# Attention beside a local branch on one core: larger PV batches, a split side branch, spare matmuls and new issue estimates

## Chip, cores, metric

One core of one Trainium2 chip. The time is the device time of one execution in us; medians of several runs are given. Profiled spans are some 2 us shorter than the timed figure of the same run. Most comparisons below are ratios to the kernel before, timed in the same rounds on the same chip: the mean time of one kernel's fast runs over that of the other's, so not quite the ratio of the medians quoted. A run counts as fast if it lies within 1.5% of the fastest of its kernel in these rounds.

## The reference, cut to what matters

```python
# shortened; x: [1, 2048, 640], 32 heads of 20
def _A_ref(x, wqkv, wo):          # full softmax attention
    scores = einsum("bhqd,bhkd->bhqk", q, k) * scale
    o = einsum("bhqk,bhkd->bhqd", softmax(scores), v)
    return heads_joined(o) @ wo
def _B_ref(x, wqkv, wo):          # each position sees 8 taps: itself and every second one before it
    logits = einsum("bhsd,bhswd->bhsw", q, kg) * scale      # masked where the tap is before the start
    o = einsum("bhsw,bhswd->bhsd", softmax(logits), vg)
    return heads_joined(o) @ wo
g = sigmoid((x * gate_w).sum(-1, keepdims=True))
return g * _A_ref(x, A_wqkv, A_wo) + (1 - g) * _B_ref(x, B_wqkv, B_wo)
```

Full attention is cut into 2048 units: one head, 128 keys, 512 queries. Each unit is one score matmul (contraction 20, in a strip of 32 rows), a share of one exponential, and one PV matmul, the product of the exponentials with V (21 output columns, in a strip of 32). The rest, called side work here, is projections, the tap branch B and the output projection ("fold").

## The kernel before

A scheduler written in Python runs while the program is built. It keeps an estimated time per engine, books every instruction with an estimated duration, and so fixes the order on each engine. On the chip only that order and the semaphores remain. Each slot `s` has three units or two in turn, with one exponential over all of them; two slots are called a pair, and the time from one pair to the next its pitch. The head is the time up to about 98 us, in which ScalarE is starved, and the tail what follows the last exponential.

```python
SEM_LAT = 0.07
...
actc = lambda n: 0.18 + n * 0.8334e-3            # booked time of an activation
...
    T("pe", 0.26, fn, reads=..., writes=[("score", s % 2)])                    # scores of a slot
    T("pe", 0.06 + 0.22 * max(1, (len(units) + 2) // 4), fn, ..., accum=["obank"])   # PV
...
for s in range(NT + 6):
    ...
    qk(s); exp(s)
    if s >= hold:                                # PV, every slot, of what the slot two back made
        todo = []
        while next_pv < NU and tile_of[next_pv][0] <= min(s - 2, NT - 1) and len(todo) < 6:
            ...
            todo.append(next_pv); next_pv += 1
        if todo: pv(todo)
    lim = exps[s - 1].end if ... else sch.avail["act"]
    run_side(lim)                                # side work that ends, by the estimate, before lim
```

Side work is written as generators that take turns. They share two PSUM banks (`side`); three and two banks hold the scores, one (`obank`) the PV sums. `gen_b(u)` is the tap branch for 256 positions: Q, K and V projections, eight products on VectorE, sums on TensorE, softmax, and eight more products; unit `u` starts when `u - 1` is done.

## Time and profile before

| | kernel before |
|---|---|
| time | 1134 us, median of 3 runs (1119 to 1134) |
| time of the execution that was profiled | 1115.7 us, not one of these three |
| profiled span, mean granted clock | 1113.9 us, 0.847 |
| first exponential starts, last one ends | 38.9 us, 1090.1 us |
| ScalarE: waits for scores | 93.6 us |

In the profile "us busy" and "idle before, releaser" per group of instructions are the columns to read; in the windows view each line is a stretch of the span, its length, the busy time and number of the instructions asked for, and the granted clock.

### The profile page before, as it was taken

To read this page: it belongs to the slowest core of one execution; us is meant where nothing else is said; L and a number is where in the kernel's file an instruction comes from. 1 tells how busy PE (TensorE), PEld (TensorE's weight loads), DVE (VectorE), ACT (ScalarE), POOL (GpSimd) and SP (SyncE) were. 2 spreads that over 40 slices of the span, in tenths; PEclk is the share of its full clock that TensorE was granted. 3 is DMA by queue.
4 is the path that set the end of the run, shared out by engine and by line. 5 is a ranking of instruction groups with operands and counts; after the bars stand their busy time and mean duration, and the time that the engine had idled before them with its cause. 6 is when DMAs were issued, how large, how long until landed. Compare 5 with 4: busy or idle time off the path is not lost.

```text
span 1113.9 us, 15049 instructions
## 1 busy us (share of the span) xinstructions
PE 1006.9 (90%) x6213; PEld 306.2 (27%) x6213; DVE 439.5 (39%) x772; ACT 960.8 (86%) x833; POOL 35.7 (3%) x26
## 2 busy tenths in 40 slices
PE   1678998999989999999999998989999989989997
PEld 0222322222323323422413332322112332322113
DVE  8315542334283542355461246364012255353102
ACT  0475999998898999998989999999998999998991
POOL 5000000004300000000000000000000000000000
PEclk9599998888898989977969997988568998976657
DMA  6310000000000000000000000000000000000000
GB/s 168 124 39 1 1 1 1 1 2 1 1 1 1 1 1 13 13 1 1 1 1 6 19 1 1 1 1 1 1 1 11 15 1 1 1 1 1 0 1 24
DMA packets 17216, 12.75 MB, mean 11 GB/s; under 512 B 11900, under 2 KB 15868, under 8 KB 17148
## 3 DMA queue, kind: packets, MB, share of 16 engines
q1 hardware_dynamic: 6268, 9.18, 2.4%
q10 hardware_dynamic: 10880, 2.62, 1.1%
q8 instruction: 48, 0.79, 0.3%
q14 instruction: 20, 0.16, 0.0%
HBM read 6.55 MB, written 2.62 MB: 8 GB/s over the span
## 4 chain that ended last, share of the span: by engine, by line
PE 63%; ACT 20%; issue 8%; DVE 6%; ACTq 2%; DMA 1%; DVEq 0%
PE side L368 25%; ACT ebuf L743 19%; PE score L730 19%; PE obank L754 18%; ACTq L290 2%; DVE stage L518 2%; DMA xT<-in_A_x_dram 1%; PE side L574 1%; PE side L528 1%; DVE vA L430 1%; DVE kT L387 1%; DVE oTt L455 1%; DVE oNt L466 1%; DVE qabs L410 0%; DVE oTn L469 0%
## 5 line engine op out<-in xcount | busy, mean ns | idle before, releaser
L743 ACT ACTIVATE ebuf<-score 128x1536 bf16<-128x1536 f32 (+1 forms) x819 | 955.3, 1253 | 98.7 <-PE score L730 93.6
L730 PE MATMUL score<-qT,kT 32*128 32x512 bf16 x2048 | 372.3, 444 | 50.4 <-ACT ebuf L743 45.3
L754 PE MATMUL obank<-ebuf,vA 128*21 128x512 bf16 x2048 | 361.4, 443 | 9.5 <-DVE vA L430 8.8
L730 PEld LDWEIGHTS score<-qT,kT 32*128 32x128 bf16 x2048 | 80.5, 93 | 318.7 <-ACT ebuf L743 211.1
L368 PE MATMUL side<-xT,kvw 128*128 128x256 bf16 (+1 forms) x760 | 142.5, 311 | 27.7 <-DMA xT<-in_A_x_dram 26.8
L754 PEld LDWEIGHTS obank<-ebuf,vA 128*21 128x21 bf16 x2048 | 75.0, 90 | 239.5 <-issue 218.2
L455 DVE STREAM_TRANSPOSE oTt<-obank 128x512 f32<-128x512 f32 x32 | 22.9, 716 | 228.8 <-PE obank L754 228.8
L368 PEld LDWEIGHTS side<-xT,kvw 128*128 128x128 bf16 x760 | 63.5, 100 | 89.3 <-issue 66.9
L368 PE MATMUL side<-xT,WqP 128*128 128x512 bf16 x160 | 58.9, 445 | 0.2
L368 PE MATMUL side<-stage,ident 128*128 128x512 bf16 (+1 forms) x192 | 55.6, 395 | 0.0
L586 DVE TENSOR_TENSOR stage<-vB,repB 128x1280 bf16<-128x1280 bf16 x64 | 50.1, 821 | 1.1
L618 DVE CAST outsb<-side 128x512 bf16<-128x512 f32 (+1 forms) x32 | 15.5, 490 | 88.7 <-PE side L368 88.7
L368 PE MATMUL side<-woA_r,oTn 128*128 128x512 bf16 (+1 forms) x256 | 50.3, 306 | 0.0
L518 DVE TENSOR_TENSOR stage<-qB,kB 128x1280 bf16<-128x1280 bf16 x64 | 48.5, 818 | 0.2
L598 DVE TENSOR_TENSOR oB<-side,rB 128x512 bf16<-128x512 f32 (+1 forms) x24 | 14.4, 602 | 79.2 <-PE side L368 79.2
L387 DVE TENSOR_SCALAR kT<-side,onesrow 128x512 bf16<-128x512 f32 x32 | 23.8, 743 | 39.0 <-PE side L368 39.0
L368 PE MATMUL side<-woBp,oB 128*128 128x512 bf16 (+1 forms) x160 | 33.9, 314 | 3.8 <-DVE oTn L469 2.8
L430 DVE CAST vA<-side 128x320 bf16<-128x320 f32 x32 | 15.7, 490 | 46.6 <-PE side L368 46.6
L368 PE MATMUL side<-kvw,xT 128*128 128x320 bf16 x160 | 32.5, 327 | 0.0
L509 DVE CAST qB<-side 128x512 bf16<-128x512 f32 (+1 forms) x24 | 14.4, 601 | 43.6 <-PE side L368 43.6
L509 DVE CAST vB<-side 128x512 bf16<-128x512 f32 (+1 forms) x24 | 14.4, 601 | 36.6 <-PE side L368 35.6
L509 DVE CAST kB<-side 128x512 bf16<-128x512 f32 (+1 forms) x24 | 14.4, 602 | 35.0 <-PE side L368 35.0
(76 smaller groups left out, 429.5 us busy)
## 6 DMA issues: line engine op xcount, KB each, us to landing
out_dram<-outsb SPq DMA_DIRECT2D x16, 160.0 KB, 1.8
stage<-in_B_wqkv_dram SPq DMA_DIRECT2D x1, 2400.0 KB, 8.8
stage<-in_A_wqkv_dram SPq DMA_DIRECT2D x1, 1600.0 KB, 6.9
kvw<-in_A_wqkv_dram SPq DMA_DIRECT2D x1, 800.0 KB, 9.4
woA_r<-in_A_wo_dram SPq DMA_DIRECT2D x4, 200.0 KB
woBp<-in_B_wo_dram SPq DMA_DIRECT2D x5, 160.0 KB
xT<-in_A_x_dram ACTq DMA_TRANSPOSE x20, 2.8
gwT<-in_gate_w_dram SPq DMA_DIRECT2D x1, 1.2 KB, 10.0
```

The source lines that it names most:

```text
L290: T("act", 6.0 + 2 * tcc, lambda e, c=c, tcc=tcc: e.dma_start_transpose(xT[:, c, tcc * 512:(tcc + 1) * 512], x_v[tcc * 512:(tcc + 1) * 512 ...
L368: ins = e.matmul(o, l, r, start=(first and i == 0), stop=(last and i == n - 1), skip_group_check=True)
L387: t = T("dve", dvc(512), lambda e, b=b, tcc=tcc: e.tensor_scalar(kT[:, q, tcc * 512:(tcc + 1) * 512], side[b][:, :], onesrow[:, 0:1], None ...
L430: t = T("dve", dvc(320), lambda e, o=o, i=i: e.tensor_copy(o, i), reads=[("side", b), "vAones"], writes=[("vA", kb, half)])
L455: T("dve", dvc(512), lambda e: e.transpose(oTt[:, :], obank[:, :]), reads=["obank"], writes=["oTt"])
L509: t = T("dve", dvc(n * TOK), lambda e, o=o, i=i: e.tensor_copy(o, i), reads=[("side", b)], writes=[key])
L518: T("dve", dvc(CN * TOK, 2), lambda e, w=w, ks=ks: e.tensor_tensor(prodB(w), qB[:, :, :], ks, ALU.mult), reads=["qB", "kB"], writes=[("pro ...
L586: T("dve", dvc(CN * TOK, 2), lambda e, w=w, vs=vs, rr=rr: e.tensor_tensor(prodB(w), vs, rr, ALU.mult), reads=["vB", ("repB", w4)], writes= ...
L618: t = T("dve", dvc(c1 - c0), lambda e, ob=ob, b=b, c0=c0, c1=c1: e.tensor_copy(ob[:, c0:c1], side[b][:, 0:c1 - c0]), reads=[("side", b)], ...
L730: ins = e.matmul(sc[:, i * 512:(i + 1) * 512], kT[32 * j:32 * j + 32, q, kb * P:(kb + 1) * P], qT[g % 3][32 * j:32 * j + 32, :], start=Tru ...
L743: exps[s] = T("act", actc(512 * n), lambda e: e.activation(ebuf[s % NE][:, 0:512 * n], score[s % 2][:, 0:512 * n], ACTF.Exp, scale=SCALE), ...
L754: ins = e.matmul(obank[32 * j:32 * j + DV, :], vA[:, kb, g % NQ, j, :], ebuf[s % NE][:, i * 512:(i + 1) * 512], start=(kb == 0), stop=(kb ...
```

## The change

The intent was to take work and changes of mode off TensorE (PV in whole groups of four, every second slot), to plan with truer durations, to keep TensorE supplied (tap projections of the next unit beside the softmax of this one), and to keep its clock up where nothing else is left to do. For the last, a spare matmul, whose result nobody reads, is put in where the plan has room before `lim`, TensorE's booked load over the last 3.4 us is under 62%, and a side bank is free. By mode I mean which part of the array a group of matmuls uses: strips of rows (scores, 32\*128 on the page), strips of columns (PV, 128\*21, and tap sums) or all of it (128\*128). In the trace before, at full clock and without idle time, the next matmul starts a median 0.315 us after one of 512 columns if the mode differs between them, and 0.216 us after it if both use all of the array. The diff is cut and in places shortened.

```diff
-SEM_LAT = 0.07
+LAT = {"pe": 0.18, "act": 0.06, "dve": 0.08, "pool": 0.1, "sp": 0.1}
+SWITCH = 0.11                                    # booked when TensorE's mode changes
-    actc = lambda n: 0.18 + n * 0.8334e-3
+    actc = lambda n: 0.08 + n * 0.8334e-3
-        T("pe", 0.26, fn, reads=..., writes=[("score", s % 2)])
+        T("pe", 0.215, fn, reads=..., writes=[("score", s % 2)], mode="row")
-        T("pe", 0.06 + 0.22 * max(1, (len(units) + 2) // 4), fn, ..., accum=["obank"])
+        T("pe", 0.215 * ((len(units) + 3) // 4), fn, ..., accum=["obank"], mode="col")
+    def filler(limit):                           # spare matmuls
+        while sch.avail["pe"] + 0.32 <= limit and sch.load(3.4) < 0.62:
+            best = [b for b in range(2) if not bank_used[b] and bank_free[b] <= sch.avail["pe"]]
+            if not best:
+                return
+            b = best[0]
+            t = T("pe", 0.215, lambda e: e.matmul(side[b][:, :], ident[:, :], xT[:, 0, 0:512], ...), ...)
+            bank_free[b] = t.end
-        if s >= hold:
+        if s >= hold and (s % 2 == 0 or s >= NT):
-            while next_pv < NU and ... and len(todo) < 6:
+            while next_pv < NU and ... and len(todo) < 12:
...
+            while todo and len(todo) % 4 and todo[-1] % 64 != 63:
+                todo.pop(); next_pv -= 1
-        lim = exps[s - 1].end if ... else sch.avail["act"]
+        lim = (exps[s - 1].end if ... else sch.avail["act"]) + (0.3, 0.15)[s % 2]
         run_side(lim)
+        filler(lim)
-    def gen_b(u): projections, then taps
+    def gen_bproj(u): projections of u, while the taps of u - 1 run
+    def gen_b(u): taps
```

More of the change, by code (lines that the diff above doesn't have):

```diff
@@ L68, in __init__ @@
         self.n = 0
+        self.mode = None
+        self.busy = []
         self.dma_final = {}
@@ L75, in ready, with load, task @@
             assert st is not None and st[0] is not None, k
-            t = max(t, st[0].end)
-        return t + SEM_LAT
-    def task(self, stream, dur, fn, reads=(), writes=(), dma=False, accum=()):
+            t = max(t, st[0].end + LAT[st[0].stream])
+        return t
+    def load(self, span):
+        t1 = self.avail["pe"]
+        tot = 0.0
+        for a, b in reversed(self.busy):
+            if b <= t1 - span:
+                break
+            tot += b - max(a, t1 - span)
+        return tot / span
+    def task(self, stream, dur, fn, reads=(), writes=(), dma=False, accum=(), mode="full"):
         deps = {}
@@ L108, in task @@
             d.mark = True
-            start = max(start, d.end + SEM_LAT)
+            start = max(start, d.end + LAT[d.stream])
+        if stream == "pe":
+            self.busy.append((start, start + dur))
+            if mode != self.mode:
+                dur += SWITCH
+                self.mode = mode
         if dma:
@@ L353, in release @@
         bank_used[b] = False
-        bank_free[b] = t.end + SEM_LAT
+        bank_free[b] = t.end + LAT[t.stream]
     def mm_group(b, mms, reads, cost, first=True, last=True, per=1):
@@ L435, in gen_gate @@
     def gen_gate(qc):
+        while qc > 1 and not done.get(("fold", qc - 2)):
+            yield ("cond",)
         b = yield from bank()
@@ L482, in gen_bweights, with gen_bproj @@
         done["bw"] = True
-    def gen_b(u):
-        qc, hu = divmod(u, 2)
+    def gen_bproj(u):
         t0 = u * TOK
-        while not (done.get("bw") and done.get(("gate", qc)) and (u == 0 or done.get(("b", u - 1)))):
+        while not (done.get("bw") and (u == 0 or done.get(("bl", u - 1)))):
             yield ("cond",)
-        while hu == 0 and qc > 0 and not done.get(("fold", qc - 1)):
-            yield ("cond",)
-        if u > 0:
-            T("dve", 0.15, lambda e: e.tensor_copy(kB[:, :, 0:PADB], kB[:, :, TOK:TOK + PADB]), reads=["kB"], writes=["kB"])
-            T("dve", 0.15, lambda e: e.tensor_copy(vB[:, :, 0:PADB], vB[:, :, TOK:TOK + PADB]), reads=["vB"], writes=["vB"])
         dst = {0: (qB, 0, "qB"), 1: (kB, PADB, "kB"), 2: (vB, PADB, "vB")}
         for m in range(3):
+            while m == 2 and u > 0 and not done.get(("bp", u - 1)):
+                yield ("cond",)
+            if u > 0 and m > 0:
+                bb, key = ((kB, "kB"), (vB, "vB"))[m - 1]
+                T("dve", 0.15, lambda e, bb=bb: e.tensor_copy(bb[:, :, 0:PADB], bb[:, :, TOK:TOK + PADB]), reads=[key], writes=[key])
             for f0 in range(0, CN, 2):
@@ L510, in gen_b @@
                 release(b, t)
+            if m == 1:
+                done[("bqk", u)] = True
+        done[("bproj", u)] = True
+    def gen_b(u):
+        qc, hu = divmod(u, 2)
+        while not (done.get(("bqk", u)) and done.get(("gate", qc)) and (u == 0 or done.get(("b", u - 1)))):
+            yield ("cond",)
         b = yield from bank()
@@ L520, in gen_b @@
             for f in range(CN):
-                yield ("pe", 0.2, sch.ready(*[("prod", half * 4 + w4) for w4 in range(4)]))
+                yield ("pe", 0.11, sch.ready(*[("prod", half * 4 + w4) for w4 in range(4)]))
                 def fn(e, f=f, half=half, b=b):
@@ L531, in fn @@
                     return ins
-                T("pe", 0.2, fn, reads=[("prod", half * 4 + w4) for w4 in range(4)] + ["Sel"],
+                T("pe", 0.11, fn, reads=[("prod", half * 4 + w4) for w4 in range(4)] + ["Sel"], mode="col",
                   **({"writes": [("side", b)]} if (half == 0 and f == 0) else {"accum": [("side", b)]}))
+        done[("bl", u)] = True
         if u == 0:
@@ L555, in gen_b @@
         T("pe", mmc(512), lambda e, b=b: e.matmul(side[b][:, :], negRep[0:32, :], m2, start=False, stop=True, skip_group_check=True),
-          reads=["mB", "negRep"], accum=[("side", b)])
+          reads=["mB", "negRep"], accum=[("side", b)], mode="row")
         yield ("act", sch.ready(("side", b)))
@@ L569, in gen_b @@
           reads=["rB", ("gB", qc % 2)], writes=["rB"])
+        while not done.get(("bproj", u)) or (hu == 0 and qc > 0 and not done.get(("fold", qc - 1))):
+            yield ("cond",)
         for w4 in range(4):
@@ L575, in gen_b @@
                                                             eB[32 * w4:32 * w4 + 32, :], start=True, stop=True),
-              reads=["eB", "Rep"], writes=[("side", b)])
+              reads=["eB", "Rep"], writes=[("side", b)], mode="row")
             yield ("dve",)
@@ L587, in gen_b @@
                   reads=["vB", ("repB", w4)], writes=[("prod", w)])
+        done[("bp", u)] = True
         for f0 in range(0, CN, 2):
@@ L738, in qk @@
             rd.add(("qT", g % 3))
-        T("pe", 0.26, fn, reads=sorted(rd, key=str), writes=[("score", s % 2)])
+        T("pe", 0.215, fn, reads=sorted(rd, key=str), writes=[("score", s % 2)], mode="row")
     def exp(s):
@@ L763, in pv @@
             rd.add(("vA", r // 4, (g % NQ) // 4))
-        T("pe", 0.06 + 0.22 * max(1, (len(units) + 2) // 4), fn, reads=sorted(rd, key=str), accum=["obank"])
+        T("pe", 0.215 * ((len(units) + 3) // 4), fn, reads=sorted(rd, key=str), accum=["obank"], mode="col")
+    def filler(limit):
[4 more added lines that the diff above has]
+            b = best[0]
+            t = T("pe", 0.215, lambda e, b=b: e.matmul(side[b][:, :], ident[:, :], xT[:, 0, 0:512], start=True, stop=True),
+                  reads=["ident", ("xT", 0, 0)], writes=[("side", b)])
+            bank_free[b] = t.end
     next_pv = 0
@@ L768, in _build @@
     HOLD = 2
-    for s in range(NT + 6):
+    SLACK = (0.3, 0.15)
+    for s in range(NT + 8):
         if next_pv >= NU:
@@ L793, in _build @@
                         add_gen(gen_b(uu), 6 + 0.01 * uu)
+                        add_gen(gen_bproj(uu), 6.5 + 0.01 * uu)
                     for qq in range(QCN):
@@ L797, in _build @@
             exp(s)
-        if s >= hold:
+        if s >= hold and (s % 2 == 0 or s >= NT):
             todo = []
-            while next_pv < NU and tile_of[next_pv][0] <= min(s - 2, NT - 1) and len(todo) < 6:
+            while next_pv < NU and tile_of[next_pv][0] <= min(s - 2, NT - 1) and len(todo) < 12:
                 g, r = divmod(next_pv, 64)
@@ L809, in _build @@
                 next_pv += 1
+            while todo and len(todo) % 4 and todo[-1] % 64 != 63:
+                todo.pop()
+                next_pv -= 1
             if todo:
@@ L813, in _build @@
                 if r == 63:
+                    if g >= NSLOT:
+                        run_until(("fold", (g - NSLOT) // NQ))
                     add_gen(gen_norm(g), 0)
                     hold = s + HOLD
-        elif s >= NT:
-            pass
-        lim = exps[s - 1].end if 1 <= s <= NT and (s - 1) in exps else sch.avail["act"]
+        lim = (exps[s - 1].end if 1 <= s <= NT and (s - 1) in exps else sch.avail["act"]) + SLACK[s % 2]
         run_side(lim)
+        filler(lim)
     run_until(("fold", QCN - 1))
```

## The prediction

> **What bounds the kernel now.** I began with the page. ScalarE is busy 86% and TensorE 90%, so either could be the bound, and the groups below show that the 819 exponentials make up all but a few us of ScalarE's 960.8.
>
> ```profile
> PE 1006.9 (90%) x6213; PEld 306.2 (27%) x6213; DVE 439.5 (39%) x772; ACT 960.8 (86%) x833; POOL 35.7 (3%) x26
> ...
> PE 63%; ACT 20%; issue 8%; DVE 6%; ACTq 2%; DMA 1%; DVEq 0%
> ...
> L743 ACT ACTIVATE ebuf<-score 128x1536 bf16<-128x1536 f32 (+1 forms) x819 | 955.3, 1253 | 98.7 <-PE score L730 93.6
> L730 PE MATMUL score<-qT,kT 32*128 32x512 bf16 x2048 | 372.3, 444 | 50.4 <-ACT ebuf L743 45.3
> L754 PE MATMUL obank<-ebuf,vA 128*21 128x512 bf16 x2048 | 361.4, 443 | 9.5 <-DVE vA L430 8.8
> ```
>
> ScalarE waits 93.6 us for scores, and the chain lies 63% on TensorE. So TensorE is mostly what sets the pace, though it has the smaller floor. To get ScalarE's floor I looked in the chain in order of time for a stretch in which it never waits:
>
> ```profile
> 1045.54 1.03 ACT ebuf L743
> ...
> 1047.80 1.03 ACT ebuf L743
> ...
> 1050.06 1.03 ACT ebuf L743
> ```
>
> A pair of exponentials (three units, then two) comes every 2.26 us. 819 of them are 409.5 pairs, 925 us, and 12 other activations at some 0.48 us add 6: a floor of **931 us** for ScalarE.
>
> Then I split the span where the granted clock changes, and asked the windows view for the exponentials alone (length, ScalarE busy, count, clock). Four full-clock stretches, three half-clock ones and the last half-clock one before the tail:
>
> ```profile
> 98.10:183.40 85.30, 80.62 (x70) 1.00 0.00 1
> 405.30:490.60 85.30, 81.77 (x70) 1.00 0.02 9
> 586.20:668.10 81.90, 79.35 (x68) 1.00 0.03 9
> 845.60:924.10 78.50, 74.88 (x65) 1.00 0.03 9
> ...
> 275.60:285.80 10.20, 6.80 (x6) 0.53 0.00 0
> 490.60:517.90 27.30, 23.24 (x21) 0.51 0.00 1
> 989.00:1019.70 30.70, 24.15 (x22) 0.51 0.00 1
> 1043.60:1090.00 46.40, 46.39 (x41) 0.50 0.00 1
> ```
>
> There are two kinds of loss. At full clock with much side work a pair takes longer than 2.26: in the first, 35 pairs in 85.3 us are 2.44. At half clock with side work 15 to 33% is idle. At half clock without side work (the last line) nothing is lost at all. TensorE's timeline at full clock shows why the first kind exists:
>
> ```profile
> 531.05 0.39 PE L730 MATMUL score<-qT,kT 32*128 32x512 bf16 x3
> 531.37 0.39 PE L754 MATMUL obank<-ebuf,vA 128*21 128x512 bf16 x3
> 531.70 0.50 PE L368 MATMUL side<-xT,kvw 128*128 128x256 bf16 x3
> 532.13 0.39 PE L730 MATMUL score<-qT,kT 32*128 32x512 bf16 x2
> 532.45 0.39 PE L754 MATMUL obank<-ebuf,vA 128*21 128x512 bf16 x2
> 532.77 0.94 PE L368 MATMUL side<-xT,kvw 128*128 128x256 bf16 x7
> 533.64 0.39 PE L730 MATMUL score<-qT,kT 32*128 32x512 bf16 x3
> ```
>
> TensorE never pauses, and a pair takes 533.64 - 531.05 = 2.59. From start to start a group of two or three scores or PVs costs 0.32, whatever is in it. A PV batch of six (two groups) takes 0.535 elsewhere in this timeline, so a further group costs 0.2135 and the remaining 0.108 is the change from one kind to the next. The old scheduler books 0.26 for scores, 0.28 for a PV batch and 2.49 for a pair of exponentials: it takes TensorE for faster and ScalarE for slower than they are, and plans more side work into a pair than fits.
>
> The accounts of this profile, 1113.9 us: first exponential at 38.9; until 98.1 a starved head (some 29 exponentials, worth 33 us, in 59); from 98.1 to 1090 the steady part, 992 us, where the other 790 exponentials and 12 activations could do with 395 x 2.26 + 6 = 899; tail 24. So **about 93 us of the steady part can be won**. Summing idle time in the windows, up to 1043.6, gives 44 us at half clock (20 stretches, 256 us) and 27 at full clock; the rest is pitch, since an exponential that starts after a gap loses its overlap with its predecessor.
>
> [...]
>
> **The change part by part.** The instruction order of the built kernel gives counts.
>
> *PV batches.* Before, 754 runs of one to three units and 32 of five to eight: 818 groups. After, 305 of four, 102 of eight, one of twelve: 512 groups. 306 x 0.2135 = **65 us less TensorE work** at full clock.
>
> *Fewer changes of mode.* Runs of one kind on TensorE fall from 2278 to 1910: 368 x 0.108 = **40 us less**.
>
> *Spare matmuls.* 232 of 512 columns: 232 x 0.2135 = **50 us more**. They stand where no side work is, four and one per pair, in four places early on and densely over the last 35 pairs or so.
>
> *Sum for TensorE at full clock.* Score groups 819 x 0.2135 = 175; PV 175, after 109; side work 655,360 columns counted in the order, at 0.2135 per 512: 273 both; changes 246, after 206; spare 0, after 50. Together 869, after 813, of which 763 are needed. Before, the granted capacity is 0.847 x 1075 us = 910: 869 is 95% of it, which is why every clumsy spell costs time. After, 763 lies well below ScalarE's 931.
>
> *New estimates.* A pair is now booked at 2.29 us, against 2.26 measured, and TensorE at 0.215 per group plus 0.11 per change, against 0.2135 and 0.108. A dense pair of the new order is scores, side x4, scores, PV x4, side x1: 8 groups of 0.2135 and 5 changes of 0.108 = 2.25 us. That no longer exceeds ScalarE. I expect 2.28 to 2.32 per pair over some 250 dense pairs: 5 to 15 us left of the pitch loss.
>
> *Two chains.* The tap branch's VectorE stage (eight products, maximum, exponential, reciprocal) leaves TensorE without side work, and half-clock stretches such as 490 to 517 and 989 to 1019 follow it. The next unit's projections now fill part of it. But there are only two side banks, and the order still has runs of five or more pairs with one side matmul each and no spare ones, because both banks are held. I expect half of the 20 half-clock stretches to stay or to turn shorter: 10 to 15 us left of the 44.
>
> *Head and tail.* The burst of side work before the second group's scores shrinks from 31 matmuls by nine of 512 columns (2 us), and PV in the first group loses some ten groups (3 us). The 0.58 us waits for V after most of its blocks stay. **5 us**. In the tail 13 matmuls of the last fold run at 0.43 instead of 0.2135 each; if the spare ones keep the clock up, 2 us come back; the norm's chain of 2.8 us stays.
>
> *Total.* 1113.9 - 93 + 10 (pitch) + 13 (clock) + 5 (transitions between groups) - 5 - 2 = 1042. The timed runs before were 1119 to 1134, above the profile's, so I allow 4 for the same in the timed runs after: **1046 us**.
>
> **Rivals.** *(a) The clock falls all the same.* Less needed work means more idle time, and spare matmuls stand in few of the tap stages. Then the half-clock loss stays near 44, and dense plans of 2.25 us at full clock meet a half clock and take over 3.5. For: the unfilled runs, and the reservation of both banks. Against: TensorE's total is smaller, and the projections spread. It would give 1075 to 1090. *(b) Spare matmuls and the slack of 0.3 and 0.15 us delay scores.* They lie ahead of scores in order and can wait for VectorE to free a bank. For: the order is fixed at build time. [...] It would cost 10 to 20 us: 1060. *(c) ScalarE becomes the only bound from the first pair on.* Then only head, tail and floor count: 1113.9 - 93 - 7 = 1014, the best possible. *(d) VectorE or bank waits take over.* VectorE is 39% busy and the work on it hardly changes, so I give this little.
>
> **Range and chances.** Between (c) at its best and (a): 1022 to 1080. To miss a gain of 2% (below 1111) nearly nothing of the 93 us would have to come back, although 105 us of TensorE work demonstrably go. I put faster at 0.94, within 2% at 0.05, slower at 0.01.
>
> **What would show it.** Right: ScalarE's waits for scores fall from 93.6 us to under 45, of which some 25 in the head; steady pairs near 2.28; PV's 2048 matmuls cover fewer groups, and the chain's ScalarE share rises above 50%; half-clock time after 98 us falls from 256 to under 130 us; the mean clock rises from 0.847 to above 0.9. Wrong: a clock that stays near 0.85 with long half-clock stretches in the tap stages (rival a); gaps ahead of scores whose releaser is VectorE or a side bank (b); aligned batches of four that take more than 0.33 us.

What the trace before shows: the clock record reads 1.00 or 0.50, and every stretch of it but the cut one at the end is a whole multiple of 3.41 us long; at 0.50 a score group takes 0.54 us from start to start, not 0.32 (1049.88 to 1050.42 us). The two or three matmuls of a group start a median 3 ns apart, and such a group takes 0.32 alike. That a batch of four costs one group too, on which the 512 groups and the 65 us rest, was the author's estimate from that; the trace after has it at a median 0.33. That less work on TensorE can cost clock (rival (a)) and that spare matmuls keep it up (the 2 us of the tail) was not shown either when this was written; experiments 6 and 1 test it. The overlap of exponentials, lost after a gap, is in the trace: of the 818 that follow another, 595 start before it ends, by a median 0.115 us.

## The result, and the profile after

| | before | after |
|---|---|---|
| time | 1131.0 us (1119 to 1134, 4 runs) | 1064.1 us (1057 to 1066, 4 runs) |
| ratio of the fast runs | | 0.9415 (0.9327 to 0.9502) |
| profiled span | 1113.9 | 1064.6 |
| mean granted clock | 0.847 | 0.894 |
| first to last exponential | 1051.2 | 1001.6 |

The change gains 6%, inside the range, 18 us short of the point. The two profiles explain 49 of the 67 us between the medians: the one before is of an execution of 1115.7 us, faster than the four runs timed beside it. The page after: busy times, the chain by engine, and the groups of exponentials, scores and PV.

```profile
PE 898.2 (84%) x6359; PEld 290.2 (27%) x6445; DVE 440.1 (41%) x772; ACT 943.9 (89%) x833; POOL 35.8 (3%) x26
...
ACT 49%; PE 31%; issue 15%; DVE 2%; ACTq 2%; DMA 1%; DVEq 0%
...
L776 ACT ACTIVATE ebuf<-score 128x1536 bf16<-128x1536 f32 (+1 forms) x819 | 939.6, 1342 | 66.2 <-PE score L763 64.5
L763 PE MATMUL score<-qT,kT 32*128 32x512 bf16 x2048 | 348.6, 419 | 116.3 <-ACT ebuf L776 107.7
L787 PE MATMUL obank<-ebuf,vA 128*21 128x512 bf16 x2048 | 200.3, 418 | 1.7 <-DVE vA L450 1.1
```

TensorE's share of the chain falls from 63 to 31%, PV's busy time from 361 to 200 us, and ScalarE's waits for scores from 93.6 to 64.5. TensorE now waits for ScalarE (107.7 us before scores, 45.3 before the change). ScalarE still waits 64.5 us. Where? The windows view of the exponentials, two full-clock stretches, then three at half clock (length, ScalarE busy, count, clock):

```profile
86.60:223.20 136.60, 136.13 (x122) 1.00 0.00 1
383.60:472.30 88.70, 88.57 (x79) 1.00 0.02 8
...
301.70:325.60 23.90, 19.36 (x17) 0.52 0.00 1
...
612.30:636.20 23.90, 19.19 (x17) 0.52 0.00 1
991.20:1011.70 20.50, 15.62 (x15) 0.52 0.00 0
```

At full clock ScalarE is now as good as never idle, and its pitch is at the floor: the timeline has 116 exponentials in one unbroken 131.21 us, 2.26 a pair. At half clock it idles as it did. Summed between the head and the last exponential, over the windows that end before the last exponential:

| | before | after |
|---|---|---|
| half clock: stretches, us, ScalarE idle | 20, 256, 44 | 24, 198, 45 |
| full clock: us, ScalarE idle | 689, 26 | 754, 3.5 |

This tally, used for half-clock time below too, leaves out the stretch in which the last exponential falls. That is 46 us more at half clock in the kernel before (49 in experiments 1 and 6), without idle time, against 2 in the changed kernel. Its cuts also lie some 0.8 us behind the changes in the clock record, which is why its half-clock stretches read 0.52 and not 0.50. Cut at the record and taken to the last exponential, half clock falls from 303 us to 201, with 41 and 39 us of ScalarE idle; at full clock the idle time is 26 and 7 us.

So the two losses that the prediction named behaved in opposite ways. The one at full clock is nearly gone. The one at half clock hardly shrank.

Even where spare matmuls stand, the clock falls. TensorE's timeline (start, duration, instructions, count, idle before) on both sides of 928.90, where the clock record falls to half for one window of 3.41 us:

```profile
924.91 0.82 PE L806 MATMUL side<-xT,ident 128*128 128x512 bf16 x3
925.67 0.39 PE L763 MATMUL score<-qT,kT 32*128 32x512 bf16 x3
925.99 0.40 PE L787 MATMUL obank<-ebuf,vA 128*21 128x512 bf16 x4
926.58 0.39 PE L763 MATMUL score<-qT,kT 32*128 32x512 bf16 x2 [0.20 <-ACT ebuf L776]
927.93 0.39 PE L763 MATMUL score<-qT,kT 32*128 32x512 bf16 x3 [0.95 <-ACT ebuf L776]
928.25 0.40 PE L787 MATMUL obank<-ebuf,vA 128*21 128x512 bf16 x4
928.90 0.61 PE L763 MATMUL score<-qT,kT 32*128 32x512 bf16 x2 [0.25 <-ACT ebuf L776]
929.43 1.89 PE L806 MATMUL side<-xT,ident 128*128 128x512 bf16 x4
```

The spare matmuls (L806) come in bursts, and for 3.7 us there is none. In the window up to 928.90 no pause is longer than 0.95 us, yet the scores that start there already run at the half rate, and the four spare ones that follow take 1.89 us, against 1.04 for such a run at full clock. In that window columns stream during 0.35 of the time.

To see what the clock goes with, I took the matmul records window by window (3.41 us each), added up the time in which columns stream (columns over the granted rate, 512 in 0.2135 us at full clock; matmuls of one group on different strips, which start some 3 ns apart, counted once), and sorted the full-clock windows by what followed:

```
full-clock windows followed by     half clock               full clock
  kernel before                    24, median 0.42 (-0.56)  194, median 0.71 (0.41-)
  changed kernel                   28, median 0.39 (-0.47)  210, median 0.68 (0.40-)
```

In these windows the clock always fell after a share below some 0.4 and always stayed after one above some 0.55; between, either happened. The longest time without a streaming column sorts the windows less well: in the changed kernel it was a median 1.13 us before half clock and 0.37 before full clock, but up to 1.14 there too. (86 of the 6445 matmuls of the changed kernel have no record; its repeat, experiment 8, and the kernel before have all, and the repeat gives 0.43 and 0.71.) This suggested that taking work off TensorE has a price of its own. The experiments test that.

### The profile page after: what moved, and what is told of

The parts are those of the page before. It is cut to its first block, busy times and chain, and to the rows that moved or that the text cites. A ratio compares the mean times of both kernels' runs of the same rounds, so it can differ in the third digit from the quotient of the medians.

```text
span 1064.6 us, 15426 instructions
## 1 busy us (share of the span) xinstructions
PE 898.2 (84%) x6359; PEld 290.2 (27%) x6445; DVE 440.1 (41%) x772; ACT 943.9 (89%) x833; POOL 35.8 (3%) x26
## 4 chain that ended last, share of the span: by engine, by line
ACT 49%; PE 31%; issue 15%; DVE 2%; ACTq 2%; DMA 1%; DVEq 0%
ACT ebuf L776 48%; PE side L388 13%; PE score L763 10%; PE obank L787 4%; PE side L806 3%; ACTq L310 2%; DMA xT<-in_A_x_dram 1%; PE side L606 0%; DVE vA L450 0%; ACT eB L588 0%; DVE outsb L651 0%; PE side L557 0%; DVE kmx L411 0%; DVE kT L407 0%; ACT gtan L462 0%
## 5 line engine op out<-in xcount | busy, mean ns | idle before, releaser
L776 ACT ACTIVATE ebuf<-score 128x1536 bf16<-128x1536 f32 (+1 forms) x819 | 939.6, 1342 | 66.2 <-PE score L763 64.5
L763 PE MATMUL score<-qT,kT 32*128 32x512 bf16 x2048 | 348.6, 419 | 116.3 <-ACT ebuf L776 107.7
L787 PE MATMUL obank<-ebuf,vA 128*21 128x512 bf16 x2048 | 200.3, 418 | 1.7 <-DVE vA L450 1.1
L388 PE MATMUL side<-xT,kvw 128*128 128x256 bf16 (+1 forms) x749 | 154.0, 322 | 29.6 <-DVE kvw L357 21.5
L806 PE MATMUL side<-xT,ident 128*128 128x512 bf16 x210 | 72.4, 448 | 2.3 <-issue 2.1
L787 PEld LDWEIGHTS obank<-ebuf,vA 128*21 128x21 bf16 x2048 | 41.9, 90 | 109.5 <-issue 104.4
L477 DVE STREAM_TRANSPOSE oTt<-obank 128x512 f32<-128x512 f32 x32 | 22.9, 716 | 112.7 <-PE obank L787 112.7
L430 DVE TENSOR_SCALAR qabs<-side 128x512 uint16<-128x512 uint16 x32 | 21.5, 673 | 89.2 <-PE side L388 89.1
L388 PE MATMUL side<-xT,WqP 128*128 128x512 bf16 x140 | 43.2, 398 | 1.6 <-issue 1.1
L436 DVE CAST qT<-side 128x512 bf16<-128x512 f32 x32 | 21.9, 684 | 27.3 <-PE side L388 21.7
L806 PEld LDWEIGHTS side<-xT,ident 128*128 128x128 bf16 x232 | 19.9, 105 | 41.6 <-issue 32.2
```

Of the source, the lines that this page charges most:

```text
L388: ins = e.matmul(o, l, r, start=(first and i == 0), stop=(last and i == n - 1), skip_group_check=True)
L430: T("dve", dvc(512), lambda e: e.tensor_scalar(qabs[:, :].bitcast(U16), side[b][:, :].bitcast(U16)[:, 1:1024:2], 0x7FFF, None, op0=ALU.bit ...
L436: t = T("dve", dvc(512), lambda e: e.tensor_copy(qT[sl][:, :], side[b][:, :]), reads=[("side", b)], writes=[("qT", sl)])
L477: T("dve", dvc(512), lambda e: e.transpose(oTt[:, :], obank[:, :]), reads=["obank"], writes=["oTt"])
L763: ins = e.matmul(sc[:, i * 512:(i + 1) * 512], kT[32 * j:32 * j + 32, q, kb * P:(kb + 1) * P], qT[g % 3][32 * j:32 * j + 32, :], start=Tru ...
L776: exps[s] = T("act", actc(512 * n), lambda e: e.activation(ebuf[s % NE][:, 0:512 * n], score[s % 2][:, 0:512 * n], ACTF.Exp, scale=SCALE), ...
```

## The experiments

Twelve kernels ran, all correct. The first four take one part out of the changed kernel; the next two put one part alone into the kernel before; the others change the spare matmuls, one of them repeating the changed kernel. Clocks and half-clock times are of one profiled run each; the repeat reads 184 us of half clock where the first profile reads 198.

**1. Without spare matmuls.**

```diff
         run_side(lim)
-        filler(lim)
```

> The changed kernel without its 232 spare matmuls. Theory: they buy little, because with them the half-clock stretches still cost ScalarE 45 us of idle time, as many as before the change (44), and where they stand no side work is waiting. Then 1060 to 1075 us against 1064. Rival: they are what keeps the clock up; without them half-clock time rises from 198 us to 300 or more and the time to 1085 or more.

1074.4 us (1070 to 1079); ratio to before 0.964 (0.956 to 0.973). Half-clock time after the head rises from 198 to 331 us (380 with the last stretch) and the mean clock falls from 0.894 to 0.807, but ScalarE's idle time in it only from 45 to 50. The rival is right on the clock and wrong on the time: most of the clock that spare matmuls save is saved where nothing needs it.

**2. PV every slot again.** The three lines of the diff that concern `s % 2`, `12` and `todo.pop()` undone; the estimates count a batch of two or three as one group.

> The changed kernel with PV issued every slot in batches of two or three as before (some 790 batches in place of 408), each booked at its true cost. Theory: the batches carry most of the gain, since they take 65 us of groups and most of 40 us of mode changes off TensorE; put back, TensorE needs near 870 us again and the plan must spread side work thinner: 1095 to 1125 us. Rival: the estimates carry it, and a plan that fits loses only the room for spare matmuls: 1065 to 1080.

1068.5 us (1059 to 1084); ratio 0.959 (0.946 to 0.972). My theory fails: undoing the batches, which I took for the largest part, costs next to nothing. The rival's 1065 to 1080 holds. The granted clock tells why (the profile is of the fastest run; the others read 0.916 to 0.936):

```profile
core 0: 1056.8 us, clock 0.950
```

With more PV groups to do TensorE streams more, a mean 0.62 of the time from 92 us to the last exponential against 0.59 in experiment 8, and the half-clock time after the head is 65 us, not 198. Only 64 spare matmuls find a place here. The work saved was also work that held the clock.

**3. The tap branch as one chain.** `gen_bproj` and `gen_b` joined again, the gate's projection as before, with the new estimates.

> The changed kernel with the tap branch as one chain (projections and taps of a unit in a row) and the gate as before. Theory: projections beside the VectorE stage fill a part of TensorE's gaps, 5 to 15 us: 1070 to 1080. Rival: two chains hold both side banks and keep spare matmuls out, so that one chain with its 303 spare matmuls is as fast or faster: 1050 to 1064.

1060.5 us (1057 to 1067); ratio 0.952 (0.943 to 0.961). The rival holds as far as it can be told: two chains gain nothing here. One chain leaves more room in the side banks for spare matmuls (303 against 232), and the half-clock time is 167 us.

**4. The old estimates.** `actc`, the latencies, the bookings of scores, PV and tap sums as before; no `SWITCH`, no slack.

> The changed kernel with the old issue estimates (a pair of exponentials booked at 2.49 us, no cost for a change of mode, no slack). Theory: the plan puts 0.2 us too much into each dense pair, so the dense pitch goes back from 2.26 to 2.45 or more over some 200 pairs: 1090 to 1110. Rival: with the smaller PV batches TensorE has room for the error and only the clock matters: 1060 to 1075.

1086.8 us (1081 to 1089); ratio 0.975 (0.966 to 0.983). The costliest part to undo, a little under what the theory said. ScalarE's idle time at full clock after 92 us is 15 us (3.0 in the changed kernel), and the half-clock stretches rise to 33. At full clock a pair takes a mean 2.35 us, against 2.27 in the changed kernel: the direction of the theory, not its 2.45.

**5. The kernel before with the estimates alone.** Latencies, mode changes, bookings and slack of the diff; nothing else.

> The kernel before with the new issue estimates and the slack alone (PV every slot, one chain, no spare matmuls). New theory after the first four: the estimates carry most of the 67 us, since undoing them cost the most (1087) and undoing the PV batches nearly nothing (1068). Then 1065 to 1085 us. Rival: the estimates help only together with the smaller PV work, 1095 to 1115.

1116.1 us (1115 to 1123); ratio 1.002 (0.993 to 1.011). Both expectations fail, the rival's by 1 us: the estimates alone gain nothing. The time from first to last exponential did fall, from 1051 to 1022 us, but the tail behind it grew from 24 to 52. TensorE's timeline shows what fell into it (the last score group is at 1058.99):

```profile
1061.59 1.59 PE L373 MATMUL side<-xT,kvw 128*128 128x256 bf16 x13
1065.02 0.72 PE L373 MATMUL side<-xT,kvw 128*128 128x256 bf16 x5 [1.84 <-DVE vB L514]
1069.26 1.26 PE L533 MATMUL side<-stage,Sel 128*32 128x256 bf16 x20 [3.52 <-DVE stage L523]
...
1088.58 6.94 PE L373 MATMUL side<-stage,ident 128*128 128x512 bf16 x24 [5.38 <-DVE stage L591]
```

These are the projections, tap sums and value sums of the last tap unit, one after the other, each waiting for VectorE. A plan that is honest about TensorE finds too little room per pair for the side work, and what does not fit is done alone at the end. Larger PV batches make that room (experiment 3 has them and one chain: tail 23 us). So do two chains (experiment 2 has them and small batches: tail 24 us). Either seems enough, and so neither is missed when it alone is taken out. This is read from the tails: neither was run with the new estimates and without spare matmuls.

**6. The kernel before with the PV batches alone.** Old estimates, one chain, no spare matmuls.

> The kernel before with the PV batches alone (old estimates, no spare matmuls). New theory: TensorE gets 65 us less to do, but streams less in each clock window, so half-clock time rises from 256 us to above 320 and eats most of it: 1100 to 1125 us. Rival, the prediction's sum: TensorE was the bound and its need falls by 100 us: 1050 to 1075.

1102.7 us (1098 to 1103); ratio 0.988 (0.980 to 0.996). As the new theory says, and far from the prediction's sum. The half-clock time after the head is 423 us, against 260 by the same tally in the kernel before (472 and 306 with the last stretch):

```profile
core 0: 1096.5 us, clock 0.777
```

**7. Spare matmuls by a finer rule, and in the bank of PV sums too.** The load is taken over 1.7 us, the mark is 80%. Where no side bank is free, the spare matmul has weights of zero and accumulates onto `obank`, which adds 0.0 to sums that are open. It is only put in where all four strips of the group have begun and the last has not ended, so that no value changes.

```diff
-        while sch.avail["pe"] + 0.32 <= limit and sch.load(3.4) < 0.62:
+        while sch.avail["pe"] + 0.32 <= limit and sch.load(1.7) < 0.80:
             best = [...]
             if not best:
-                return
+                if not 4 <= next_pv % 64 <= 60:
+                    return
+                T("pe", 0.215, lambda e: e.matmul(obank[:, :], zrow[:, :], xT[:, 0, 0:512],
+                                                  start=False, stop=False, skip_group_check=True),
+                  reads=["zrow", ("xT", 0, 0)], accum=["obank"])
+                continue
```

> The changed kernel with spare matmuls wherever TensorE's last 1.7 us were less than 80% full by the plan; where no side bank is free they multiply by zero weights and add that to the bank of PV sums, which changes no value (506 in side banks, 219 of zeros). Theory: the 45 us of idle time at half clock come from windows in which less than some 0.45 of the time is streamed, and filling them evenly removes most: half-clock time under 80 us after the head, 1025 to 1045 us. Rival: it is the side work's place, not the clock, that starves ScalarE, or more spare matmuls delay the scores: 1060 or more. If zeros do not count as work for the clock, the tap stages stay at half clock: about 1050.

**1009.1 us (1007 to 1010)**; ratio 0.904 (0.895 to 0.913). Better than the theory's range, and the fastest kernel. The page and the windows view of the exponentials (head, then the rest):

```profile
PEclk9798999999999999999999999999999999999999
...
L778 ACT ACTIVATE ebuf<-score 128x1536 bf16<-128x1536 f32 (+1 forms) x819 | 931.1, 1444 | 20.1 <-PE score L765 20.1
```

```profile
39.10:92.00 52.90, 39.63 (x34) 0.90 0.24 78
92.00:985.00 893.00, 891.37 (x785) 1.00 0.01 3
```

From 92 us on ScalarE is idle 1.6 us of 893, and there is no half-clock window. The kernel sits at ScalarE's floor, with 725 more matmuls than the work needs, 493 more than the changed kernel. Its 277 full-clock windows that were followed by another stream a median 0.74 and at least 0.46. The matmuls by zero did hold the clock here. Counted without them, eight of these windows stream only 0.26 to 0.39, with them 0.58 to 0.79, and all eight are followed by full clock; in both kernels above no window under 0.40 was. The zeros stand in the tap stages among the other side work, as the timeline shows:

```profile
480.94 0.40 PE L789 MATMUL obank<-ebuf,vA 128*21 128x512 bf16 x4
481.27 0.39 PE L390 MATMUL side<-xT,kvw 128*128 128x256 bf16 x2
481.60 0.39 PE L765 MATMUL score<-qT,kT 32*128 32x512 bf16 x2
481.92 0.50 PE L390 MATMUL side<-xT,kvw 128*128 128x256 bf16 x3
482.26 0.59 PE L808 MATMUL obank<-xT,zrow 128*128 128x512 bf16 x2
```

It also shows the batch of four at its price: 0.33 from its start to that of the next.

**8. The changed kernel again**, on the chip of experiments 5 to 7.

> The changed kernel once more, on the chip of these three, as their measure: 1055 to 1068 us.

1063.1 us (1061 to 1067); ratio 0.953 (0.945 to 0.962). It repeats, and it is the measure for the others.

**9. The finer rule in side banks alone.** Experiment 7 without its second half.

> As the 1009 us version, with the spare matmuls in side banks alone (468 of them, none of zeros): the finer rule by itself. Theory: the rule, 80% over 1.7 us in place of 62% over 3.4, mends the thin windows in stretches without side work, and the places in the bank of PV sums mend the tap stages, half and half: 1030 to 1045 us. If the rule is all: 1005 to 1015. If the places are all: 1055 or more.

1049.1 us (1043 to 1056); ratio 0.940 (0.930 to 0.950). Just above the range of "half and half": against 1063, the rule brings at most some 14 us, and its interval overlaps that of experiment 8. The places in the bank of PV sums bring the other 40. In the profile 167 us of half clock are left after the head, and the mean clock is 0.909, against 0.990 in experiment 7: the gaps that mattered are those in which both side banks are held.

**10. The kernel before with these spare matmuls alone.**

> The kernel before with that rule for spare matmuls and nothing else of the change (240 in side banks, 30 of zeros). Theory: the clock holds better, but the old estimates overfill dense pairs at 2.59 us, and little room is left for spare matmuls: 1075 to 1105 us. If the clock alone were the matter: 1045 to 1065.

1073.7 us (1071 to 1082); ratio 0.961 (0.951 to 0.971), the clock at 0.964. 270 spare matmuls and nothing else gain 3.9%, against 4.7 (experiment 8) to 5.9% for the whole change. This lies just under the theory's range. ScalarE still waits 66.0 us for scores, though from some 135 us on the page's clock row reads 9 in every slice. The trace agrees with the theory that the old estimates overfill: at full clock a pair takes a mean 2.38 us, and 418 of 788 take over 2.35, against 2.27 and 33 of 783 in experiment 7. No run of its own separates it.

**11. Experiment 7 with one chain.**

> The 1009 us version with the tap branch as one chain. Theory: once the clock holds, the places of the projections hardly matter: 1005 to 1015 us. Rival: two chains are needed to fit the side work beside the exponentials: 1020 or more, with a tail above 24 us.

1012.7 us (1012.5 to 1012.9); ratio 0.907 (0.900 to 0.914), tail 22.9 us. The same within the intervals. With batches and a held clock two chains are not needed.

**12. Experiment 7 with PV every slot.**

> The 1009 us version with PV every slot in twos and threes. Theory: once the clock holds, TensorE's need at full clock is some 870 us of about 1000 and the batches still give room: with them undone 1015 to 1035 us. Rival: the batches gave nothing that a held clock doesn't: 1005 to 1012.

Four runs: 1033, 1034, 1051, 1067; median 1043; the profile fell on the slowest, so I do not read it. The two fast ones give a ratio of 0.926 (0.913 to 0.939) and lie in the theory's range; the median does not. The two slow ones had the lower clock, 0.942 and 0.959 against 0.982 and 0.983. With the finer spare matmuls the batches are worth some 24 us by the fast runs (1033 against 1009), 34 by the medians, against 5 without (experiments 2 and 8).

## Why the prediction was right or wrong

The time, the sign and the range were right; the two parts of the gain were not of the sizes given.

**What bounds the kernel.** Right: floor, pitch and half-clock loss were read from the kernel before, and experiment 7 brought ScalarE's busy time to 934.4 us, within 4 us of the floor of 931. Rival (c), "the best possible" at 1014, was reached by a kernel I had not thought of.

**"I expect 2.28 to 2.32 per pair ... 5 to 15 us left of the pitch loss."** Better than that: 2.26 in unbroken runs, and 3.5 us of idle time at full clock by the tally (7 by the record). The new estimates are needed for it (experiment 4), as is room in the pair (experiment 5).

**"I expect half of the 20 half-clock stretches to stay or to turn shorter: 10 to 15 us left of the 44."** This step failed: 24 stretches, 45 us left (39 of 41 by the clock record). The head, with 5 predicted, gave about 12 (before: 29 exponentials, worth 33 us, in the 59 from 38.9 to 98.1, 26 lost; after: 34, worth 38, in the 53 from 39.8 to 93.0, some 14 lost); the clock record has 24 us of the head at half clock before and 10 after, and whether that is the cause was not tested. The steady part gave 37 (93 before; after 948 us from 93.0 to 1041.3 for 785 exponentials and 11 activations, worth 892, so 56 lost), where I had 65. That sum, 37 + 12 and 0.5 in the tail, is the 49.3 us by which the profiled spans differ; the prediction's span of 1042 us was missed by 23. The miss at half clock, some 30 us, was in part made good by a pitch and a head some 13 us better than predicted: as the total goes, that is luck.

Why it failed is shown. I counted less work on TensorE as gain alone ("After, 763 lies well below ScalarE's 931") and had no share of work at which the clock stays. The traces gave one, 0.4 to 0.55 of a window, and experiment 6 the consequence: 306 groups fewer, 423 us of half clock in place of 260. Rival (a) described the mechanism, but as an alternative to the gain; it was at work beside it. Its guess that both banks are held was the right place to look: experiments 7 and 9 differ mainly in that, 40 us. Its 1075 to 1090 did not come.

**Parts.** The prediction's terms for batches (65 us of work) and mode changes (40 us) were of the right size, and the batch was priced rightly (0.33 for four units). Its 2278 and 1910 changes include those between two kinds of matmul of one mode, which cost nothing like 0.108 (the next full matmul of 512 columns starts 0.216 to 0.226 us after). By the weight loads in the traces the mode changes 2100 and 1742 times, 358 fewer, 39 us; its sums of 869 and 813 are some 18 us too high, their difference is not. But work off TensorE is not time: by itself 1.2% (experiment 6), and hardly to be told when undone (experiment 2). The terms also are no sum. Estimates alone are worth 0% and cost 2% when undone; batches and chains stand in for each other. Rival (b), that slack and spare matmuls delay scores, is refuted by experiment 7, where with 725 spare ones and the same slack ScalarE idles 1.6 us of 893. Rival (d) is not seen ahead of the scores, which after the change wait for ScalarE for 107.7 of their 116.3 us.

**The signs I named.** Met: fewer PV groups, batches of four at 0.33, pairs of 2.26 where dense. Missed: waits for scores 64.5 us (under 45), half-clock time 198 us (under 130), clock 0.894 (above 0.9), ScalarE's share of the chain 49% (above 50). They pointed to the clock, as they were meant to.

**Open.** Whether the mark of 62% with the extra places would have been enough was not tried. How much of the 40 us between experiments 9 and 7 the zeros brought is not quite isolated: experiment 7 also has 38 more spare matmuls in side banks. The spread of the runs (1105 to 1136 us before, 0.4 us in experiment 11) goes with the clock (0.855 and 0.819 in those two runs before); why the clock differs from run to run was not shown.

## What to carry to other kernels

Where the granted clock depends on how much TensorE streams, as it did here (full-clock windows followed by half clock streamed a median of 0.39 to 0.42 of the time, those followed by full clock 0.68 to 0.71), work taken off TensorE is a gain only if what is left still holds the clock, or if nothing needs TensorE's speed in that stretch (as in the last 46.40 us of exponentials before the change, at half clock, with ScalarE busy for 46.39): look at the clock window by window before counting it. Fill thin windows evenly and everywhere (median time and profiled clock: 1009 us and 0.990 in experiment 7, 1049 us and 0.909 without the places in the bank of PV sums); a matmul with zero weights onto an open accumulation needs no buffer of its own (219 of them in experiment 7). And a plan fixed at build time needs true costs as well as room: with true costs alone, what does not fit is only moved to the end (experiment 5: the tail grew from 24 to 52 us).
